# Attention beside a Mish MLP on one core: a stricter rule for ScalarE side jobs, and the row maxima of the two array halves kept level

## The chip, the cores and the metric

The kernel runs on one core of one Trainium2 chip. The metric is device time in microseconds (us), the median of three runs. TensorE (PE in the profile) multiplies, ScalarE (ACT) evaluates functions and copies, VectorE (DVE) reduces and adds, GpSimd (POOL) does elementwise work on data in on-chip memory, and SyncE (SP) issues the DMAs. Each engine works through its own list of instructions in order, and semaphores order the lists against each other.

## The reference

```python
xn = layernorm(x)                               # x: 2048 x 512, D = 512
q = (xn @ wq) in 32 heads of 16;  k = xn @ wk;  v = xn @ wv      # one k and one v for all heads
s = softmax(q k^T / 4) v, heads joined, @ wo
h = xn @ w1 + b1                                # 512 -> F = 1792
g = silu((h * tanh(softplus(h))) @ w2)          # Mish, then back to 512
out = x + s * g
```

All is float32. The softmax needs, for every head and query, the maximum of a row of 2048 scores, and then the exponentials and their weighted sum.

## The kernel before, in words

**Units and steps.** The 2048 queries are cut into 4 chunks of 512 and the 32 heads into 8 groups of 4, so that there are 32 units (chunk, group). A unit takes 16 steps, one for every 128 keys, and there are 512 steps. A head is only 16 deep, and its rows stand several times (high and low parts), so that a score matmul needs 64 of the 128 rows of the TensorE array or fewer: two heads of a unit lie in the lower 64 rows ("side 0") and two in the upper 64 ("side 1"), and a matmul on one side can run beside one on the other.

**What a step issues.** Three kinds of half-array matmul, all of 512 columns:

- "e" (line 1039, in `e_one`): four score tiles, each followed by an exponential on ScalarE (line 1041). In the main loop, all four e of step s lie on the one side 1 - s % 2.
- "m" (line 1060, in `m_one`): score tiles for the row maxima of a unit `LEAD` = 20 steps ahead; VectorE reduces each (line 1064, tile mb). `m_next[0]` and `m_next[1]` count how many have been issued on each side. Four m per step on the average.
- "x" (line 118, in `Mm.half`): the dense layers (queries, w1, w2, wo). Their matmuls are 128 rows deep and are issued as two halves: the halves on side s % 2 in one step, the other halves, on the other side, in the next one. A group of 12 or 15 such matmuls fills one PSUM bank (xps); `chunk_size` cuts it into chunks of at most `XMAX` = 8: 12 into 6 and 6, 15 into 8 and 7. One chunk of k matmuls thus takes two steps. The groups of 15 are those of the second dense layer for the first two of the three parts of F in `THIRDS`, four per chunk of queries and part: 32 in all.

Each step ends with the full-height matmuls "pv" (line 1122), which weigh the values of the step two before; they need all rows.

**How a step is put together.** `m_sides` decides how many of the step's m (`tot` = 4; with odd k, 5 in the chunk's first step and 3 in its second) go to the side of the e (n) and how many to the side of the x (the rest), from k and within limits that keep the two counts at most `MLAG` = 4 apart:

```python
        n = max(min((k + tot - 4) // 2 if k % 2 else k // 2, hi), lo)
        return n, tot - n
```

`em` puts the e and the n m of their side in a row as "MEMEMEME"; `waves` then emits in turn one x of the one side and one e or m of the other, keeps the last of the e side until the last x, and emits the rest of the m, which share the rows of the x, after the x (for odd k after everything). The first x half of the next step waits for the exponential or reduction that followed the last of the other side (`cur["relay"]`), so that the two halves never add into the bank together.

**ScalarE's side jobs.** Beside the exponentials ScalarE evacuates the banks of the dense layers (lines 716, 776, 845) and runs side jobs that wait in the queue `jobs`: the exponentials and logarithms of Mish, of the silu and of the softmax denominators (lines 784, 793, 797, 859, 867, 872, 1146, 1150). `act_jobs` is called once in a step, after the step's e and m. It runs one job, or two when more than two wait; in a step with a bank evacuation on ScalarE (`gap[0]`) it runs one if more than two wait and none otherwise.

**The end.** From step 492 on (`NS - LEAD`) there are no m left. The steps are taken in pairs (`late_pair`), each with eight e and up to two dense groups in "lanes", of each of which 3 to 5 matmuls are done, both halves; `next_group` fills a lane. A group that the main loop left unfinished goes into a lane with what is left of it. After step 512 the last groups and the output follow.

The planning is done when the program is built, with the kernel's own estimates of the times; the engines' lists of instructions are then fixed.

Of the kernel before, what the change touches and what calls it, by code (L numbers as in the profile page):

```python
# [62 lines left out]
def m_need(v):  # L63

    return (34, 64)[v] if v < 2 else 32 * (v + 1)
# [59 lines left out]
def block_kernel(ctx: ExitStack, tc: tile.TileContext, x, wq, wk, wv, wo, w1, b1, w2, out):  # L125
# [169 lines left out]
    def x_high(t):  # L295
        act.activation(x_part(t, 0), xp_of[t], AF.Copy)
# [3 lines left out]
    def x_copy(t):  # L300
        c, tt = divmod(t, 4)
        if tt == 0:
            xf_of[c] = [sb.tile([P, 2, C], F32, tag="act", name=f"xf{c}_{k}", bufs=NACT) for k in range(2)]
        for k in range(2):
            act.activation(xf_of[c][k][:, :, P * tt:P * (tt + 1)], xp_of[t][:, 2 * k:2 * k + 2], AF.Copy)

    def x_low(t):
        sub(dve, x_part(t, 1), xp_of[t], f(x_part(t, 0)))
# [54 lines left out]
    jobs = deque()  # L363
# [5 lines left out]
    gap = [0]  # L369
    ran = [0]  # L370

    def act_jobs(n):
        n = (int(len(jobs) > 2) if gap[0] else n) if n < 9 else n
        gap[0] = 0
        while n > 0:
            k = next((k for k, (fn, free) in enumerate(jobs)
                      if free is None or free() is not None and free() <= step[0]), None)
            if k is None:
                return
            fn = jobs[k][0]  # L380
            del jobs[k]
            fn()
            n -= 1
            ran[0] += 1
# [97 lines left out]
    def pump():  # L482
        for tag in items:
            while arrived(tag):
                split(tag)
            load(tag)
# [3 lines left out]
    cur = {"g": None, "ps": None, "n": 0, "chunk": [], "relay": None}  # L490

    def is_ready(g):
        return (all(i.tile is not None and i.ready <= step[0] + g.slack(k) for k, i in enumerate(g.items))
                and all(d() is not None and d() <= step[0] for d in g.after) and g.pre is None)

    def prepare():
        for n in range(min(2 if step[0] < NS - LEAD else 8, len(queue))):
            if queue[n].pre and queue[n].pre():
                queue[n].pre = None
# [37 lines left out]
    def fill(quota):  # L537
        while quota > 0:
            if cur["g"] is None and not begin():
                return  # L540
            g = cur["g"]
            n = min(quota, len(g.mms) - cur["n"])
            for m in g.mms[cur["n"]:cur["n"] + n]:
                m(cur["ps"])
            cur["n"] += n
            quota -= n
            if finish():
                return
# [3 lines left out]
    lanes = [None, None]  # L552
# [3 lines left out]
    def next_group(z):  # L556

        if cur["g"] is not None:
            lanes[z] = [cur["g"], cur["n"], cur["ps"], None]
            cur["g"] = None  # L560
            return
        prepare()
        if not queue or not is_ready(queue[0]):
            return
        g = queue.popleft()
        if g.start:
            g.start()
        if g.alloc:
            ps = g.alloc(z)
        else:  # L570
            assert not (z and lent)
            ps = late_banks[0] if z else ps_x.tile([P, 512], F32, tag="x", name="xps")
        lanes[z] = [g, 0, ps, None]
# [454 lines left out]
    def e_one(s, i):  # L1028

        v, r = divmod(s, 16)  # L1030
        if s < NS - LEAD:
            a, k, p = 1 - s % 2, r - r % 2 + i // 2, i % 2
        else:
            a, k, p = i % 2, r, i // 2
        q = qt_of[v]
        o = 64 * a
        n_e[0] = (n_e[0] + 1) % (5 if len(lent) < 2 else 4) if late_banks else 0
        e = late_banks[5 - n_e[0]] if n_e[0] > 2 else ps_e.tile([P, C], F32, tag="e", name=f"e{s}_{i}")
        pe.matmul(e, ks[o:o + 64, P * k:P * (k + 1)], q[o:o + 64, p], start=True, stop=True)  # L1039
        pt = sb.tile([P, C], F32, tag="pt", name=f"pt{s}_{i}", bufs=NPT)  # L1040
        r = act.activation(pt, e, AF.Exp, scale=0.25)  # L1041
        pt_of[16 * v + k, p, a] = pt
        return r
# [28 lines left out]
    def m_sides(h, k, second):  # L1072

        tot = 4 + (0 if k % 2 == 0 else -1 if second else 1)
        tot = min(tot, 64 * NU - sum(m_next))
        ahead = m_next[h] - m_next[1 - h]
        lo = max((tot - MLAG - ahead + 1) // 2, tot - (32 * NU - m_next[1 - h]), 0)
        hi = min((tot + MLAG - ahead) // 2, 32 * NU - m_next[h], tot)
        n = max(min((k + tot - 4) // 2 if k % 2 else k // 2, hi), lo)
        return n, tot - n  # L1080

    def c_rows(v):
# [126 lines left out]
    def due(t):  # L1209
        step[0] = t  # L1210
        for k in sorted(k for k in timed if k <= t):
            for fn in timed.pop(k):
                fn()
# [23 lines left out]
    def task(eng, us, fn, deps=(), **kw):  # L1237
        t = Task(eng, us, fn, deps, **kw)
        plan[eng].append(t)
        return t  # L1240
# [57 lines left out]
    for c0, c1 in ((0, 1), (1, 2), (2, 3), (3, 4)):  # L1298
        z = slice(4 * c0, 4 * c1)
# [3 lines left out]
        for c in range(c0, c1):  # L1303
            xs, scs = [], []
            for t in range(4 * c, 4 * c + 4):
# [3 lines left out]
                if c == 0:  # L1309
                    hi = task("ACT", 0.55, lambda t=t: x_high(t), [tr])  # L1310
                    lo = task("DVE", 0.65, lambda t=t: x_low(t), [hi])
# [5 lines left out]
                else:  # L1317
                    lo = task("ACT", 0.62, lambda t=t: x_copy(t), [tr])
# [66 lines left out]
    while True:  # L1385
# [21 lines left out]
        s, e, k = min(opts, key=lambda o: o[0])  # L1407
# [36 lines left out]
        elif k == "J":  # L1444
            tag = next((g for g in ("wq", "ws", "wb") if (g == "wq" or s > 19.0) and arrived(g) and busy[0] + E0 < s + 0.5), None)
            n = ran[0]
# [16 lines left out]
    while left:  # L1463
        k = next(k for k in left if all(d.end is not None for d in k.deps))
# [8 lines left out]
    def pv_to(s):  # L1473

        while pv_next[0] <= s:
            k = pv_next[0]
            pv(k)
            pv_next[0] += 1
            if k % 16 == 15:
                o_out(k // 16)  # L1480
                return

    for s in range(NS + 2000):
        inm = s < NS - LEAD
        if inm or cur["chunk"]:
            assert s < NS
            due(s)
            h = s % 2

            def em(k, second):  # L1490
                n, rest = m_sides(1 - h, k, second) if inm else (0, 0)
                x = deque(lambda i=i: e_one(s, i) for i in range(4))
                y = deque(lambda: m_one(1 - h) for _ in range(n))
                r = [[], []]
                for op in EM if k % 2 == 0 or second else EM[::-1]:
                    if op == "M" and y:
                        r[1 - h].append(y.popleft())
                    elif op == "E":
                        r[1 - h].append(x.popleft())
                r[h] = [lambda j=j: m_one(h, n + rest > 4 and j == rest - 1) for j in range(rest)]  # L1500
                return r

            if s >= 2 and (s - 1) % 16 == 0 and s > 1:
                gap[0] += 1
            waves(h, em, s < NS - LEAD - 1)
            act_jobs(1 + (len(jobs) > 2))
            due(s + 0.5)
            pv_to(s - 2)
        elif s < NS:
            due(s)  # L1510
            if not late_banks:
                late_banks.extend(ps_m.tile([P, C], F32, tag="m", name=f"late{k}") for k in range(3))
                if (NS - s) % 2:
                    for i in range(4):
                        e_one(s, i)
                    fill(4)
                    act_jobs(1)
                    pv_to(s - 2)
                    step[0] = s
                    continue  # L1520
            if (NS - s) % 2 == 0:
                late_pair(s)
            else:
                if s < NS - 3:
                    act_jobs(1)
                pv_to(s - 1)
        else:
            due(s)
            if s == NS:
                act_jobs(2)  # L1530
                pv_to(NS - 1)
                due(s + 0.5)
                lanes_end()
                fill(3)
                fill(3)
            fill(16)
            act_jobs(100)
        step[0] = s
        if vdone[0] < 8 * NC and min(m_next) >= m_need(vdone[0]):
            r = c_rows(vdone[0])  # L1540
            rowq.extend([lambda r=r: (r[0](), behind.append(r[1])),
                         lambda r=r: (r[2](), behind.append(lambda: (r[3](), r[4]())))])
            vdone[0] += 1
        if rowq and not evacs[0]:
            rowq.popleft()()
        while behind and s >= NS - LEAD - 1:
            behind.popleft()()
        evacs[0] = 0
        pump()
        if s > NS + 1 and not queue and cur["g"] is None and not timed and not jobs:  # L1550
            break
# [12 lines left out]
```

## Time and profile before

| | us |
|---|---|
| median of three runs (lowest to highest) | 1581.02 (1580.65 to 1581.16) |
| the profiled execution's own time | 1580.51 |
| its span, first to last instruction | 1578.7 |

| engine | busy in the span, us | share |
|---|---|---|
| TensorE, matmuls | 1566.1 | 99% |
| TensorE, weight loads (beside the matmuls) | 842.6 | 53% |
| VectorE | 1341.9 | 85% |
| ScalarE | 1306.6 | 83% |
| GpSimd | 626.4 | 40% |

In a row of the timeline stand the start in us from the span's start, the length in us, the engine ("PEld" are weight loads), the line, the operation, the tile written and those read, the shapes, the count of instructions merged in the row, and in brackets the idle time before it with what ended it. A row of the waits has the total in us, the number of waits and the longest. A row of the groups has the count, the busy time in us, the mean of one in ns, and the idle time before them.

### The profile page before, as it was taken

The page shows a single profiled execution, that of the slowest core. Times are in us where ns is not written, and L with a number is a line of the kernel's source. Part 1 is how long each engine was busy: PE and PEld are TensorE (multiplying, and loading weights), DVE is VectorE, ACT ScalarE, POOL GpSimd, SP SyncE. Part 2 cuts the span into 40 slices and gives each one's busy share as a digit, 9 for nine tenths or more (in the row PEclk, how much of TensorE's full clock was granted, in tenths as well). Part 3 has the DMA queues.
Part 4 walks back from the last instruction along what each step waited for, and adds up shares of the span by engine and source line. Part 5 has one row for each costly group of instructions (what it writes and reads, how often), then busy time and mean ns, then how long its engine had stood idle before and what let it go on. Part 6 is the DMA issues. An engine that isn't in the chain of part 4 may idle for free.

```text
span 1578.7 us, 31652 instructions
## 1 busy us (share of the span) xinstructions
PE 1566.1 (99%) x11717; PEld 842.6 (53%) x11717; DVE 1341.9 (85%) x2341; ACT 1306.6 (83%) x2515; POOL 626.4 (40%) x641
## 2 busy tenths in 40 slices
PE   9999999999999999999999999999999999999998
PEld 5455555555555555555555555555555555555554
DVE  8998888889889888888898988888889998888832
ACT  7488798798998778978988787897898878789886
POOL 3476266274474104613525131362252414225412
PEclk9999999999999999999999999999999999999999
DMA  6233221132321304222122312220332213032011
GB/s 195 94 117 112 65 100 43 55 125 84 124 91 47 103 15 151 58 71 67 39 79 71 109 61 62 81 71 16 124 98 85 69 54 102 18 111 58 15 58 51
DMA packets 74666, 124.31 MB, mean 79 GB/s; under 512 B 21520, under 2 KB 35344, under 8 KB 74512
## 3 DMA queue, kind: packets, MB, share of 16 engines
q1 hardware_dynamic: 74512, 122.29, 25.1%
q8 instruction: 93, 1.52, 0.4%
q14 instruction: 61, 0.50, 0.1%
HBM read 74.78 MB, written 26.21 MB: 64 GB/s over the span
## 4 chain that ended last, share of the span: by engine, by line
PE 96%; DVE 2%; ACT 1%; DMA 0%; SPq 0%; issue 0%; POOL 0%; ACTq 0%; DVEq 0%
PE xps L118 44%; PE pv L1122 32%; PE e L1039 8%; PE m L1060 8%; DVE mb L1064 2%; PE kp L319 1%; PE xps L114 0%; ACT pt L1041 0%; PE xp L287 0%; PE late L118 0%; DMA xin<-in_dram 0%; PE late L1039 0%; PE wop L114 0%; DVE xt L162 0%; SPq L224 0%
## 5 line engine op out<-in xcount | busy, mean ns | idle before, releaser
L1064 DVE TENSOR_REDUCE mb<-m 128x1 f32<-128x512 f32 x2048 | 1274.0, 683 | 175.0 <-PE m L1060 153.4
L1041 ACT ACTIVATE pt<-e 128x512 f32<-128x512 f32 x2018 | 1061.9, 603 | 219.3 <-PE e L1039 210.6
L1060 PE MATMUL m<-ks,qt 48*128 48x512 f32 (+1 forms) x2048 | 830.5, 421 | 1.7 <-DVE mb L1064 0.8
L1039 PE MATMUL e<-qt,ks 64*128 64x512 f32 x2018 | 741.2, 401 | 0.5 <-ACT pt L1041 0.3
L1122 PE MATMUL pv<-pt,vaug 128*32 128x512 f32 x4096 | 543.0, 604 | 0.0
L1060 PEld LDWEIGHTS m<-ks,qt 48*128 48x128 f32 (+1 forms) x2048 | 372.5, 185 | 63.0 <-DVE mb L1064 25.3
L1039 PEld LDWEIGHTS e<-qt,ks 64*128 64x128 f32 x2018 | 373.3, 186 | 18.5 <-ACT pt L1041 6.7
L118 PE MATMUL xps<-wbs,act 64*128 64x512 f32 x1248 | 338.1, 407 | 0.1
L118 PEld LDWEIGHTS xps<-wbs,act 64*128 64x128 f32 x1248 | 217.6, 185 | 172.2 <-ACT pt L1041 100.7
L118 PE MATMUL xps<-xt,ws 64*128 64x512 f32 x1104 | 306.0, 410 | 0.1
L118 PEld LDWEIGHTS xps<-xt,ws 64*128 64x128 f32 x1104 | 190.2, 185 | 183.2 <-ACT pt L1041 116.5
L172 POOL TENSOR_SCALAR t<-t 128x512 f32<-128x512 f32 x56 | 34.4, 614 | 329.3 <-ACT t L784 328.9
L1122 PEld LDWEIGHTS pv<-pt,vaug 128*32 128x32 f32 x4096 | 81.9, 108 | 136.9 <-issue 128.8
L162 POOL TENSOR_TENSOR hb<-hb,t 128x512 f32<-128x512 f32 x56 | 72.3, 1290 | 64.2 <-ACT t L797 44.1
L118 PE MATMUL xps<-xt,wq 64*128 64x512 f32 x336 | 93.2, 410 | 0.0
L118 PEld LDWEIGHTS xps<-xt,wq 64*128 64x128 f32 x336 | 57.9, 185 | 55.5 <-ACT pt L1041 35.2
L118 PE MATMUL xps<-wbs,ot_all 64*128 64x512 f32 x288 | 79.5, 408 | 0.0
L118 PEld LDWEIGHTS xps<-wbs,ot_all 64*128 64x128 f32 x288 | 49.5, 184 | 46.4 <-ACT pt L1041 30.2
L162 POOL TENSOR_TENSOR hb<-hb,u 128x512 f32<-128x512 f32 x56 | 72.3, 1291 | 4.4
L162 POOL TENSOR_TENSOR u<-u,t 128x512 f32<-128x512 f32 x56 | 71.8, 1282 | 4.7
L162 POOL TENSOR_TENSOR act<-hb,act 128x512 fp32r<-128x512 f32 x55 | 70.8, 1287 | 4.6
L162 POOL TENSOR_TENSOR oc<-oc,sc 128x512 f32<-128x512 f32 (+1 forms) x16 | 20.6, 1288 | 116.5 <-ACT sc L1150 72.0
(146 smaller groups left out, 945.6 us busy)
## 6 DMA issues: line engine op xcount, KB each, us to landing
wbs<-w SPq DMA_DIRECT2D x36, 512.0 KB
ws<-w SPq DMA_DIRECT2D x35, 512.0 KB
qt<-qh SPq DMA_DIRECT2D x256, 32.0 KB
wq<-wq SPq DMA_DIRECT2D x14, 512.0 KB
w<-wbs SPq DMA_DIRECT2D x14, 512.0 KB
wbs<-wo SPq DMA_DIRECT2D x12, 512.0 KB
rawws<-in_dram SPq DMA_DIRECT2D x21, 256.0 KB
rawwb<-in_dram SPq DMA_DIRECT2D x20, 256.0 KB
```

The costliest lines, as they stand in the source:

```text
L118: i = self.pe.matmul(ps, self.lhs()[o], self.rhs()[o], start=(self.k == 0 and self.halves == 0), stop=(self.k == self.tot - 1 and self.hal ...
L162: eng.tensor_tensor(out=o, in0=a, in1=b, op=op)
L172: pool.tensor_scalar(o, o, lim, 0.0, op0=ALU.min, op1=ALU.max)
L319: pe.matmul(kp_of[c], wkf[:, dt], xf_of[c][dt // 2][:, dt % 2], start=(dt == 0), stop=(dt == 3))
L1039: pe.matmul(e, ks[o:o + 64, P * k:P * (k + 1)], q[o:o + 64, p], start=True, stop=True)
L1041: r = act.activation(pt, e, AF.Exp, scale=0.25)
L1060: pe.matmul(m, q[o, p, P * t:P * (t + 1)], ks[o, C * kb:C * (kb + 1)], start=True, stop=True)
L1064: r = dve.reduce_max(out=mb_of[v][:, kb, z:z + 1], in_=m, axis=AX.X)
L1122: pe.matmul(o[32 * j:32 * j + 32], vaug[:, k], pt, start=(k == 0), stop=(k == 15))
```

## The change

Three things are changed. First, in `act_jobs` and at its call in the main loop, "more than two wait" becomes "more than three wait". Second, `m_sides` gets a correction: n is first chosen as before; then it is worked out by how much the step would leave the side of its e ahead in m, less two where the e are on side 1 (h = 1 in `m_sides`) and nothing where they are on side 0; where a chunk of x is in the step (k > 0) and this differs from zero by more than one, n is moved by one towards it. Third, a group that goes from the main loop into a lane takes along the instruction for which its next half has to wait.

```diff
     def act_jobs(n):
-        n = (int(len(jobs) > 2) if gap[0] else n) if n < 9 else n
+        n = (int(len(jobs) > 3) if gap[0] else n) if n < 9 else n
...
     def next_group(z):
...
         if cur["g"] is not None:
-            lanes[z] = [cur["g"], cur["n"], cur["ps"], None]
+            lanes[z] = [cur["g"], cur["n"], cur["ps"], cur["relay"]]
...
     def m_sides(h, k, second):
...
-        n = max(min((k + tot - 4) // 2 if k % 2 else k // 2, hi), lo)
+        n = (k + tot - 4) // 2 if k % 2 else k // 2
+        off = ahead + 2 * n - tot - 2 * h
+        if k and abs(off) > 1:
+            n -= 1 if off > 0 else -1
+        n = max(min(n, hi), lo)
         return n, tot - n
...
             waves(h, em, s < NS - LEAD - 1)
-            act_jobs(1 + (len(jobs) > 2))
+            act_jobs(1 + (len(jobs) > 3))
             due(s + 0.5)
             pv_to(s - 2)
```

## The prediction

> **What bounds the kernel now.** I read the page first: the busy shares, the granted clock and the chain of waits.
>
> ```profile
> span 1578.7 us, 31652 instructions
> PE 1566.1 (99%) x11717; PEld 842.6 (53%) x11717; DVE 1341.9 (85%) x2341; ACT 1306.6 (83%) x2515; POOL 626.4 (40%) x641
> PEclk9999999999999999999999999999999999999999
> PE 96%; DVE 2%; ACT 1%; DMA 0%; SPq 0%; issue 0%; POOL 0%; ACTq 0%; DVEq 0%
> ```
>
> TensorE is in the chain for 96% of the span, at full clock, and is almost never without a matmul. That a matmul is always running doesn't yet say that both halves of the array are in use, so the next thing to read is the timeline of single steps. A step's end shows as its pv row (x8); the distance of two such rows is a step. Here are two ordinary steps (six x halves) and the two after them:
>
> ```profile
> 747.32 1.07 PE L1122 MATMUL pv<-pt,vaug 128*32 128x512 f32 x8
> 750.12 0.68 ACT L776 ACTIVATE hb<-xps,b1c 128x512 f32<-128x512 f32 x1
> 750.17 1.06 PE L1122 MATMUL pv<-pt,vaug 128*32 128x512 f32 x8
> 751.64 0.74 ACT L793 ACTIVATE t<-u,two 128x512 f32<-128x512 f32 x1
> 752.25 2.08 ACT L1041 ACTIVATE pt<-e 128x512 f32<-128x512 f32 x4
> 753.35 1.06 PE L1122 MATMUL pv<-pt,vaug 128*32 128x512 f32 x8
> 756.34 1.07 PE L1122 MATMUL pv<-pt,vaug 128*32 128x512 f32 x8
> ```
>
> The first takes 2.85 us. The second takes 3.18 and the third 2.99: ScalarE had an evacuation and a side job behind one step's exponentials, then more jobs, and the exponentials start late. That is the stall the job rule is about. Now a stretch with chunks of eight, in which one step happens to be lopsided:
>
> ```profile
> 538.05 1.06 PE L1122 MATMUL pv<-pt,vaug 128*32 128x512 f32 x8
> 540.09 0.39 PE L118 MATMUL xps<-wbs,act 64*128 64x512 f32 x1
> 540.09 0.39 PE L1039 MATMUL e<-qt,ks 64*128 64x512 f32 x1
> 540.09 0.42 PEld L118 LDWEIGHTS xps<-wbs,act 64*128 64x128 f32 x2
> 540.32 0.39 PE L118 MATMUL xps<-wbs,act 64*128 64x512 f32 x1
> 540.55 0.63 PE L118 MATMUL xps<-wbs,act 64*128 64x512 f32 x2
> 541.02 0.63 PE L1060 MATMUL m<-ks,qt 48*128 48x512 f32 x2
> 541.45 1.29 DVE L1064 TENSOR_REDUCE mb<-m 128x1 f32<-128x512 f32 x2 [0.55 <-PE m L1060]
> 541.58 1.06 PE L1122 MATMUL pv<-pt,vaug 128*32 128x512 f32 x8
> ...
> 544.32 0.39 PE L118 MATMUL xps<-wbs,act 64*128 64x512 f32 x1
> 544.33 0.40 PE L1039 MATMUL e<-qt,ks 64*128 64x512 f32 x1
> 544.65 0.64 PE L1122 MATMUL pv<-pt,vaug 128*32 128x512 f32 x4
> ```
>
> Two starts that belong together (540.09, one on each side) are a slot; the next starts 0.23 us later (540.32, 540.55). Starts on one side with no partner also take 0.23 each. The step from 541.58 to 544.65 has eight x against four e and four m, eight slots, 3.07 us. An ordinary one has six x and one m against four e and three m, seven slots, 2.85 us: one slot less, 0.22 less. The step from 538.05 to 541.58 has the limit of `MLAG` at work: n = 2, so ten half matmuls (eight x, two m) against six. It lasts 3.53 us: two slots more, 0.46 more. So a step's price is 1.24 us (pv and the edges) plus 0.23 us times the longer side's count.
>
> The whole loop agrees:
>
> ```profile
> 86.71 1.06 PE L1122 MATMUL pv<-pt,vaug 128*32 128x512 f32 x8
> 89.55 1.06 PE L1122 MATMUL pv<-pt,vaug 128*32 128x512 f32 x8
> ...
> 475.17 1.06 PE L1122 MATMUL pv<-pt,vaug 128*32 128x512 f32 x8
> ...
> 478.08 0.64 PE L1122 MATMUL pv<-pt,vaug 128*32 128x512 f32 x4
> ...
> 1506.02 1.06 PE L1122 MATMUL pv<-pt,vaug 128*32 128x512 f32 x8
> 1509.42 1.06 PE L1122 MATMUL pv<-pt,vaug 128*32 128x512 f32 x8
> ```
>
> From the first row to the last are 489 steps and 1422.7 us. Four are without x (two of them 2.91 us, ending at 478.08, and 3.40, ending at 1509.42; the other two 2.71), together 11.7 us. The other 485, counted by the code's rule, are 391 of seven slots, 92 of eight, one of six and one of ten: 3489 slots. 485 x 1.24 + 3489 x 0.23 = 1403.9 us, against 1411.0 measured. All stalls of the loop on other engines are thus about 7 us, and that is the most that smoother side jobs can win.
>
> **The level rule, which is the large term.** With six x the old n (3) makes the sides differ by two and by nothing in turn, which is what the rule wants: off is 0. With seven, off is 1 or less: left alone. With eight, n = 4, and off = 0 + 8 - 4 - 2 = 2 on side 1, and the same from the other side in the next step (-2 + 8 - 4 - 0 = 2): n becomes 3. A step that had eight against eight now has seven (four e, three m) against nine (eight x, one m). The order of the changed program's instructions shows it: x7 and x8 stand together, then the last e, then one m on the rows of the x, then pv. Nine slots for eight, and no matmul fewer.
>
> How many: 31 of the 32 groups of fifteen begin in the loop, each with a chunk of eight over two steps, 62 steps of which one is the lopsided one. In the changed program's order all 32 begin there, 64 steps: 62 with nine slots, one with ten, one with eight. 62 x 0.23 = **+14.3 us**. What could cover it: nothing on TensorE, since pv needs all rows and follows the ninth slot. The m moved from the seventh slot to the ninth is reduced 0.46 us later, but VectorE is behind TensorE by less than a step:
>
> ```profile
> L1064 DVE TENSOR_REDUCE mb<-m 128x1 f32<-128x512 f32 x1962 | 1221.0, 683 | 172.3 <-PE m L1060 151.1 <-PE xps L118 19.4 <-PE e L1039 0.2
> ```
>
> Four of 683 ns are 2.73 us in a step that now lasts 3.30. In the ten-slot step two reductions ended after pv had begun (541.45 + 1.29), and the next still took 3.07. The fourth e stays in slot eight, so ScalarE and the wait of the next x for its exponential (`cur["relay"]`) are no later against the step's end.
>
> **The other corrections.** After the first empty step three steps of six x are moved by one, eight slots for seven: 3 x 0.23 = **+0.7**. The two steps of four x at the very start get seven slots for six; the second of them, from 86.71 to 89.55 in the rows above, already takes 2.84, as long as seven slots, so I take nothing (two slots, 0.5, at most).
>
> **A group that moves.** In the changed order the loop has two empty steps instead of four, and two more steps of chunks of eight (3.07 each; their ninth slot is in the 62). Out go 2.91 + 3.40 = 6.3, in come 6.1: **-0.2**.
>
> **The job rule.** Seven steps of the loop have two jobs, seven an evacuation and a job; afterwards none and three. The place shown costs 3.18 + 2.99 - 2 x 2.85 = 0.47. Counting the pv distances, the like places lose 2.0 us in all (two of 0.47, four of 0.24, one of 0.13), and the three that remain, at 0.24, 0.7: **-1.3**. A job later by a step could delay a group, but by the changed order none is: the loop does one group more, not less, and the side jobs are the same 248.
>
> **The last 20 steps.** One lane begins with a group of which eight matmuls are done, so three pairs have four matmuls in a lane where they had five: one slot less in each of two halves. From the rows of the scores that open a pair:
>
> ```profile
> 1516.57 0.50 PE L1039 MATMUL e<-qt,ks 64*128 64x512 f32 x1
> ...
> 1521.85 0.49 PE L1039 MATMUL e<-qt,ks 64*128 64x512 f32 x1
> ...
> 1532.16 0.50 PE L1039 MATMUL late<-qt,ks 64*128 64x512 f32 x2
> ...
> 1537.02 0.49 PE L1039 MATMUL e<-qt,ks 64*128 64x512 f32 x2
> ```
>
> a pair with a lane of five takes 5.28, one with four 4.86: 3 x 0.42 = -1.3 at most, nothing if the eight exponentials (some 0.6 each) and a job set the pair. I take **-1.1**. The lane that is carried over has a new wait, for an exponential of the step before, with all of TensorE behind it. The loop has this wait at every chunk, and it costs TensorE next to nothing there:
>
> ```profile
> PE xps L118 <- ACT pt L1041: 0.3, 1, 0.3
> ```
>
> so 0, and one exponential, 0.6, at most.
>
> **Sum.** 14.3 + 0.7 - 0.2 - 1.3 - 1.1 = +12.4 us. On the profiled execution's 1580.5 (span 1578.7 and 1.8 around it) that is 1592.9; the median lies 0.5 above that execution, so **1593.4 us**, 0.8% slower. Bounds: if every stall in the loop vanished (-7.1 for the -1.3), 1587.6; with nothing won from jobs and lanes and 0.6 + 0.5 lost at the lane and the four-x steps, 1596.9.
>
> **Rivals.**
>
> *The ninth slot is hidden.* ScalarE's exponentials would have to set the end of a step of eight, not the slots: four exponentials (2.1) and a job (0.74) are 2.8 of 3.07. Then the first term is 0, the sum -1.9, and the time 1579.1: no slower than before. It decides if a ninth slot costs under 0.08 us (62 x 0.08 = 5, less 1.9, is 0.2% of the time, about what a measurement of this kernel can tell from no change). Against it: two extra slots cost 0.46 in the one lopsided step, and eight slots cost just one more than seven. With the stalls of the steps of seven gone too (another 2), it would be 1577, faster. Chance 0.05, of it 0.02 faster.
>
> *Partly hidden.* The longer steps give ScalarE and VectorE time to catch up, and the steps after them run at the bare price; 0.15 to 0.2 us a slot net. 62 x 0.16 = 9.9, the sum about +8, 1589. For it: some steps of seven take up to 0.1 over the price. Chance 0.13.
>
> *Weights on the same side can't load under a matmul.* x8 follows x7, and m follows x8, on the same rows with nothing between; if the load (0.18 us a row) had to wait for the running matmul, an extra slot would cost 0.41, and the sum would be 62 x 0.18 = 11.2 more: 1604.6. Against it: in the lopsided step two loads on the same rows take 0.42 together, under the running x, whose starts stay 0.23 apart. The Trainium skill ("TensorE: Matmul & The Clock Gate", Part 3) says that a weight load overlaps with running matmuls only where the row group differs; this trace disagrees. Chance 0.03.
>
> *The delayed jobs come back as stalls*, at the lanes or after step 512, where a job is waited for. Two or three exponential-sized jobs, 2 us: 1596. The jobs left at step 510 are one in both orders. Chance 0.05, in the range.
>
> The forecast itself has 0.74, with its own range 1590 to 1596. The range for 8 in 10 takes in the partly hidden case and late jobs: **1587 to 1597**. Faster 0.02, the same 0.04, slower 0.94.
>
> **What will show it.** Right: pv rows 3.30 apart in the steps of eight x, with an unpaired x and an unpaired m in each; 2.85 in the steps of six; busy time per engine but for TensorE unchanged; the first pv of the last 20 steps some 13 us later. Wrong: pv rows still 3.07 apart there (the ninth slot is free), or 3.5 (loads don't overlap); a new idle time of TensorE ended by a side job's line; or a last part longer than the 69 us from 1509.42 on.

## The result, and the profile after

The changed kernel takes 1593.43 us (median of six runs, 1593.16 to 1593.79) against 1581.03 before: ratio 1.0073, 95% interval 1.0059 to 1.0087. The forecast was 1593.4, in a range of 1587 to 1597.

The page of the changed kernel's profile, its span, its busy shares, its granted clock and the chain by engine:

```profile
span 1591.7 us, 31648 instructions
PE 1579.7 (99%) x11717; PEld 853.3 (54%) x11717; DVE 1346.3 (85%) x2339; ACT 1307.5 (82%) x2515; POOL 627.3 (39%) x641
PEclk9999999999999999999999999999999999999999
PE 96%; DVE 2%; ACT 1%; DMA 0%; SPq 0%; issue 0%; ACTq 0%; DVEq 0%
```

The same 11717 matmuls keep TensorE busy for 13.6 us longer; their weight loads, beside them, 10.7; no other engine has grown by more than 4.4. That is what slots without a partner look like on a page: as many matmuls, a longer union of their times, and not more idle time (12.6 us of the span before, 12.0 after). The timeline shows where. It is the end of one step of eight x and the whole of the next (the columns are those of the timelines before):

```profile
125.31 1.06 PE L1126 MATMUL pv<-pt,vaug 128*32 128x512 f32 x8
...
127.35 0.42 PEld L118 LDWEIGHTS xps<-wbs,act 64*128 64x128 f32 x2
127.56 0.39 PE L1039 MATMUL e<-qt,ks 64*128 64x512 f32 x1
127.58 0.40 PE L118 MATMUL xps<-wbs,act 64*128 64x512 f32 x1
127.80 0.45 PE L1039 MATMUL e<-qt,ks 64*128 64x512 f32 x1
127.81 0.63 PE L118 MATMUL xps<-wbs,act 64*128 64x512 f32 x2
128.28 0.39 PE L1060 MATMUL m<-ks,qt 64*128 64x512 f32 x1
128.61 1.07 PE L1126 MATMUL pv<-pt,vaug 128*32 128x512 f32 x8
...
131.58 0.39 PE L1060 MATMUL m<-ks,qt 64*128 64x512 f32 x1
131.90 1.06 PE L1126 MATMUL pv<-pt,vaug 128*32 128x512 f32 x8
```

The row at 127.81 is two x, 0.23 us apart, and the m at 128.28 starts 0.24 after the second: the ninth slot, with the other side empty. pv follows it. The steps last 3.30 and 3.29 us.

The engine's waits are as short as before; no wait has taken the place of another. The first row is of the kernel before, the other two of the changed kernel:

```profile
PE m L1060 <- DVE mb L1064: 0.8, 3, 0.3
...
PE m L1060 <- DVE mb L1064: 0.5, 1, 0.5
PE xps L118 <- ACT pt L1041: 0.3, 1, 0.3
```

Put together from the pv rows of the two profiled executions (1578.7 and 1591.7 us of span):

| part of the span | before, us | after, us | difference |
|---|---|---|---|
| to the first pv | 86.7 | 87.9 | +1.2 |
| 489 steps of the loop | 1422.7 | 1436.3 | +13.6 |
| last 20 steps, to the last pv | 54.5 | 53.1 | -1.4 |
| from the last pv to the end | 14.8 | 14.4 | -0.4 |

Within the loop: the 62 steps of nine slots take 3.302 us on the average, where steps of eight x and eight slots took 3.084: 62 x 0.218 = +13.5. The three corrected steps of six x take 3.09 for 2.86, +0.7. The group that moved: two steps of eight x (6.2) for two without x (5.9), +0.3. The one step of four x in this stretch, +0.4. The rest, -1.3, is what the stalls of the loop have become less.

### The profile page after: what moved, and what is told of

It is laid out like the page before. It is cut to its first block, busy times and chain, and to the rows that moved or that the text cites. A ratio compares the mean times of both kernels' runs of the same rounds, so it can differ in the third digit from the quotient of the medians.

```text
span 1591.7 us, 31648 instructions
## 1 busy us (share of the span) xinstructions
PE 1579.7 (99%) x11717; PEld 853.3 (54%) x11717; DVE 1346.3 (85%) x2339; ACT 1307.5 (82%) x2515; POOL 627.3 (39%) x641
## 4 chain that ended last, share of the span: by engine, by line
PE 96%; DVE 2%; ACT 1%; DMA 0%; SPq 0%; issue 0%; ACTq 0%; DVEq 0%
PE xps L118 46%; PE pv L1126 32%; PE m L1060 8%; PE e L1039 7%; DVE mb L1064 2%; PE kp L319 1%; ACT pt L1041 1%; PE late L118 1%; PE xps L114 0%; PE xp L287 0%; DMA xin<-in_dram 0%; PE late L1039 0%; PE late L114 0%; PE wop L114 0%; DVE xt L162 0%
## 5 line engine op out<-in xcount | busy, mean ns | idle before, releaser
L1039 PE MATMUL e<-qt,ks 64*128 64x512 f32 x2018 | 732.1, 401 | 0.5 <-ACT pt L1041 0.3
L157 POOL TENSOR_SCALAR qh<-qf 128x512 fp32r<-128x512 f32 x15 | 9.3, 621 | 106.0 <-ACT qf L716 80.0
```

The costliest lines, as they stand in the source:

```text
L157: pool.tensor_scalar(o, i, 1.0, 0.0, op0=ALU.mult, op1=ALU.add)
```

## The experiments

All times are medians; the kernel before took 1580.92 us beside the first four and 1580.75 beside the last three.

**The level correction left out in steps of eight x.** Against the changed kernel:

```diff
-        if k and abs(off) > 1:
+        if 0 < k < 8 and abs(off) > 1:
```

> The changed kernel with the level correction left out in the steps of eight x, and only there. In its order all 62 steps with nine slots have eight again; 3538 slots against 3600; everything else stands in the same steps. Theory: 62 x 0.22 = 13.6 less than the changed kernel, 1579.8 us. Rival (the ninth slot is hidden): no change, 1593. Rival (half hidden, the rest is from the other corrections): 1586 to 1588.

Measured: 1580.11 us (ten runs, 1579.25 to 1580.48), 13.3 less than the changed kernel; ratio to the kernel before 0.9994 (0.9985 to 1.0004), no change that can be told. 13.3 / 62 = 0.215 us a slot, of the 0.23 between two starts: the ninth slot was paid almost in full, and it is the whole loss.

**Two slots without a partner.** The kernel before with the third change, and in place of the correction:

```diff
+        if k == 8:
+            n -= 2
```

> The kernel before with n = 2 in every step of eight x: six half matmuls on the side of the e, ten on the side of the x, so two slots without a partner in each of 62 steps and one or two in a step of seven x; the order of all else is that of the kernel before. Theory (every slot without a partner costs the same 0.22 to 0.23, first or second): 62 x 2 x 0.22 = 27.3 more than before, 1608.3 us (1609.6 at 0.23). Rival (weights on the same side can't load under a running matmul, so that a slot without a partner costs 0.4): 1631. Rival (one slot is covered by ScalarE's and VectorE's slack and only the next is paid): +14, 1595.

Measured: 1608.26 us, +27.3, as the first theory has it. The steps of ten slots take 3.54 us, 0.46 over those of eight. Neither the first nor the second slot is covered, and loading weights under a running matmul on the same rows costs nothing extra; 1595 and 1631 are both excluded.

**The level correction alone** (the changed kernel with "more than two" for the jobs):

```diff
-        n = (int(len(jobs) > 3) if gap[0] else n) if n < 9 else n
+        n = (int(len(jobs) > 2) if gap[0] else n) if n < 9 else n
...
-            act_jobs(1 + (len(jobs) > 3))
+            act_jobs(1 + (len(jobs) > 2))
```

> The changed kernel with the old job rule (more than two wait); the level correction alone. In its order 60 steps of eight x have nine slots, one step of seven x has nine for eight, the two steps of four x at the start have seven for six, and nothing else moves. Theory: 60 x 0.22 + 0.2 + 0.2 + 0.8 at the start = +14.4, about 1595.4 us, 2 more than the changed kernel. Rival (late jobs are the cause): near 1581. Rival (the longer steps win time back on ScalarE where the old job rule stalls): 1593 or less.

Measured: 1593.65 us, the same as the changed kernel and 1.8 under what was expected. The stalls of the loop (its 489 steps' times less 1.24 + 0.23 for each slot, steps without x left aside) are 5.5 us here and 7.1 before. At 0.22 us a slot, which the kernel of ten slots gives, the difference is 1.0 and not 1.6. Either way some time comes back with the longer steps, as the third possibility said. Beside the level correction the job rule is worth 0.2 us between the medians and 0.7 between the two profiled executions (1594.18 and 1593.44).

**The job rule alone** (the changed kernel without the correction):

```diff
-        if k and abs(off) > 1:
-            n -= 1 if off > 0 else -1
```

> The changed kernel without the level correction (n as before the change); the job rule (more than three) and the carried lane stay. In its order the loop has 3534 slots against 3526 before, two steps without x instead of four, no step with two jobs, and three with an evacuation and a job instead of seven. Theory (slots at 0.23 us plus small gains): two more steps of eight (+6.1), two of the steps without x less (-6.1), one slot each in two steps (+0.5), stalls -2.0, last 20 steps and what follows -1.9: about 1577.7 us, some 3 less than before. Rival (the change is slow because delayed side jobs hold groups up, not because of the slots): near 1593, since all jobs are as late here as in the changed kernel.

Measured: 1587.28 us (1585.39 to 1588.29), ratio 1.0039 (1.0024 to 1.0054): slower than before, where a gain of 3 had been expected. The rival as written (jobs hold groups up) isn't it either: the groups stand in the same steps as in the kernel of the first experiment, which takes 1580.1. The waits of TensorE name another cause, new in this kernel:

```profile
PE e L1039 <- DMA qt<-cr: 5.0, 3, 1.7
```

Three times the first scores of a unit wait for the transfer that writes the unit's row maxima into its query tile. The timeline at the first of them (unit 9, whose first step follows the pv at 495.06):

```profile
486.41 0.68 DVE L162 TENSOR_TENSOR y<-xps,y 128x512 f32<-128x512 f32 x1
...
490.59 0.25 DVE L1091 TENSOR_REDUCE mp<-mb 128x16 f32<-128x64 f32 x1
...
494.38 0.20 DVE L1103 STREAM_TRANSPOSE cr<-mp 128x32 f32<-128x32 f32 x1
...
494.61 5.31 SPq L1111 DMA_DIRECT2D qt<-cr  x8
...
495.06 1.07 PE L1124 MATMUL pv<-pt,vaug 128*32 128x512 f32 x8
...
498.49 0.46 PE L1039 MATMUL e<-qt,ks 64*128 64x512 f32 x1 [1.71 <-DMA qt<-cr]
```

The maxima are put together at 490.59 and turned at 494.38; eight DMA issues follow, which take 5.3 us; the unit's step begins at 496.06, and its first e starts at 498.49, 3.9 after the first issue. The step takes 5.00 us. Those of units 13 and 15 take 6.17 and 4.98: with this one 7.6 over three ordinary ones. The wait is nearly the same in all three (1.71, 1.62 and 1.68); the step of unit 13 is longer because TensorE's granted clock fell behind the wait. Its slots are 0.42 to 0.43 us apart, and the next step takes 3.28. In these rows (units 9 and 13) stand a stretch and its length, the busy time of the five engines, the granted clock, the DMA engines' share and GB/s:

```profile
495.06:500.06 5.00, 3.29 (x24) 1.61 (x22) 2.82 (x6) 2.06 (x6) 0.00 (x0) 1.00 0.03 6
685.21:691.38 6.17, 4.55 (x24) 2.38 (x22) 3.33 (x7) 2.01 (x5) 0.00 (x0) 0.76 0.02 3
```

So a part of the loss in this execution is lost clock, some 1.2 us in the step. It may also be why the four executions lie so far apart: at 1585.39 and 1586.53 us the mean clock is 0.999, at 1588.29 and 1588.04 it is 0.996; only the first has a trace. In the kernel without the correction in steps of eight x, the same unit's first step begins after the pv at 497.15:

```profile
486.85 0.27 DVE L1093 TENSOR_REDUCE mp<-mb 128x16 f32<-128x64 f32 x1
488.48 0.68 DVE L162 TENSOR_TENSOR y<-xps,y 128x512 f32<-128x512 f32 x1
...
493.62 0.20 DVE L1105 STREAM_TRANSPOSE cr<-mp 128x32 f32<-128x32 f32 x1
493.85 5.31 SPq L1113 DMA_DIRECT2D qt<-cr  x8
...
497.15 1.07 PE L1126 MATMUL pv<-pt,vaug 128*32 128x512 f32 x8
```

There the issues begin 4.3 us before the unit's step (493.85 to 498.15), not 1.5 (494.61 to 496.06): the last maximum comes a step earlier, so that the maxima are begun before the addition y out of the bank, not after. The order agrees: `rowq` is held back in a step that ends such an addition (`evacs[0]`). With an odd number of steps without x, the chunks begin in the other kind of step, and the last maximum of a unit comes four steps ahead of the unit instead of five; where the next step also holds the queue back, it is too late. Neither is enough alone: in the kernel before, units 11 to 30 have the short lead too, units 5 and 7 are held back, their issues begin 4.1 to 4.5 us ahead of their steps, and none of them waits. Two ways to lose this lead are told apart by the next two kernels.

**The sides level also without x.** The job rule alone, and

```diff
+        if k == 0 and step[0] < 480:
+            n = 2
```

> The kernel with the job rule alone, and with n = 2 in the two steps without x, so that no step leaves the sides further apart than an ordinary one. In its order there is no step of nine or ten slots, the last maximum of units 9 to 21 still comes four steps ahead of the unit's first scores (five in the changed kernel), and in units 9, 13 and 15 the step that would begin the writing of the maxima into the query tile (line 1109 before the change) is one with an addition out of a bank on VectorE, which puts it off by one more step. Theory A (the phase: the row of maxima starts a step later, and a step later again behind the addition): the stalls at the first scores of units 9, 13 and 15 stay, 7 to 8 us, and the time is that of the job rule alone, 1585 to 1588 us. Theory B (the sides are four apart, and that is what holds the maxima up): the stalls go, 1578 to 1580.

Measured: 1589.57 us (1586.23 to 1589.87), with three waits for the same transfer. Theory A stands for the waits: how far the sides are apart isn't their cause. Its figure is exceeded by 1.6 us. Two things were left out of it. Each of the two steps without x takes 3.40 us here, where it takes 2.70 with the job rule alone: +1.4. And the clock fell behind all three waits, not one. At unit 9 the step with the wait and the next one are:

```profile
495.81:501.30 5.49, 3.79 (x25) 1.78 (x23) 3.28 (x7) 2.42 (x6) 0.00 (x0) 0.89 0.03 6
501.30:505.20 3.90, 3.90 (x24) 1.79 (x23) 2.61 (x6) 1.83 (x5) 1.27 (x1) 0.71 0.45 137
```

The three steps with a wait and the three after them take 28.3 us here, 25.1 in the profiled execution of the job rule alone.

**The maxima not held back.** The job rule alone, and

```diff
-        if rowq and not evacs[0]:
+        if rowq:
```

> The kernel with the job rule alone, and with one condition dropped in the main loop: the maxima of a finished unit are put together and written (the queue rowq) also in a step with an addition out of a bank on VectorE, instead of waiting for the next step. No matmul, job or slot moves. Theory A (the write of the maxima is late by the step it is put off): the waits for the transfer at units 9, 13 and 15 go, 8 us less than the job rule alone, 1577 to 1579 us. Rival (the transfer itself is slow there, or the issue queue full): 1585 or more. Rival (VectorE, with the addition and the maxima in one step, holds up TensorE instead): 1580 to 1583.

Measured: 1578.48 us (eleven runs, 1577.98 to 1579.36), 8.8 less than the job rule alone; ratio to the kernel before 0.9987 (0.9978 to 0.9996). The waits for the transfer are gone. The timeline at unit 9, whose first step follows the pv at 495.60:

```profile
486.77 0.68 DVE L162 TENSOR_TENSOR y<-xps,y 128x512 f32<-128x512 f32 x1
...
488.57 0.25 DVE L1091 TENSOR_REDUCE mp<-mb 128x16 f32<-128x64 f32 x1
...
492.08 0.20 DVE L1103 STREAM_TRANSPOSE cr<-mp 128x32 f32<-128x32 f32 x1
492.31 5.30 SPq L1111 DMA_DIRECT2D qt<-cr  x8
...
495.60 1.06 PE L1124 MATMUL pv<-pt,vaug 128*32 128x512 f32 x8
```

The maxima are put together 1.8 us after the addition begins, not 4.2, and the issues begin 4.3 us before the unit's step. With the waits the fall of the clock behind them is gone as well. This version is faster than the changed kernel and, by 0.13%, than the kernel before; it lies near the 1577.7 us that had been expected of the job rule alone.

**The level correction in steps of fewer than eight x, from the fifth step on.**

```diff
-        if k and abs(off) > 1:
+        if 0 < k < 8 and step[0] > 4 and abs(off) > 1:
```

> The changed kernel with the level correction only in steps of fewer than eight x and from the fifth step on: three steps of six x have eight slots, and nothing else is corrected. Theory: the kernel without the correction in steps of eight (1580.1), less 0.8 us for the two steps of four x at the start, which then are as before: 1579.3 us, 1.7 less than before the change. If the first scores still come 0.7 us later in the span than before the change, that part of the start is not the correction's. Rival (the corrections at the start cost nothing, the start differs from run to run): 1580.1.

Measured: 1579.08 us (eleven runs), 1.0 less than with the two steps at the start; 0.9992 (0.9983 to 1.0001) of the kernel before. In the profiled executions the two steps at the start take 0.8 us less (0.44 and 0.35). The first scores come 0.85 us earlier besides, at 78.43 us of the span, and a wait for weights in one later step (3.62 us) takes some 0.5 back. So of the 1.0 us it isn't shown how much is the correction's and how much the earlier start's.

## Why the prediction was right, point by point

- *The sum, +12.4.* Between the two profiled executions the time grew by 12.9 us (1580.51 to 1593.44), their spans by 13.0. That the forecast meets the median to the tenth is luck: the errors of the terms below (-0.8, +0.5, -0.7, +1.6) nearly cancel, and the median before lay 0.5 above its profiled execution, the median after did not.
- *The ninth slot, +14.3.* Right in mechanism and nearly in size: 13.5 in the trace, 13.3 between two kernels that differ in this alone. The price read off one lopsided step and off the difference between seven and eight slots held for all 62.
- *The other corrections, +0.7.* Right for the three steps of six x (+0.7). For the steps of four x at the start the forecast took nothing, with 0.5 at most, because the second of them was already as long as seven slots; this term was mis-sized, and the two lose 0.8. Another 0.75 is lost ahead of them (the last point below). The pv rows of the changed kernel

```profile
87.90 1.07 PE L1126 MATMUL pv<-pt,vaug 128*32 128x512 f32 x8
91.12 1.06 PE L1126 MATMUL pv<-pt,vaug 128*32 128x512 f32 x8
```

 are 3.22 apart, 0.38 more than before, and the step ahead loses another 0.45. An m has moved ahead of the third e there. The m have three banks, so the fourth m of these steps waits for a reduction, and the e wait behind it. In the first of the two steps VectorE reduces without a pause; in the second it had been idle for 0.7 us before, and the m simply come faster than it reduces them:

```profile
86.48 1.03 PE L1060 MATMUL m<-ks,qt 64*128 64x512 f32 x2
...
87.35 0.62 PE L1039 MATMUL e<-qt,ks 64*128 64x512 f32 x2
...
89.93 0.79 PE L1060 MATMUL m<-ks,qt 64*128 64x512 f32 x2
90.56 0.63 PE L1039 MATMUL e<-qt,ks 64*128 64x512 f32 x2
```

 What the prediction didn't see is that a step pays for the order of its m, and not only for its slots, where VectorE has no slack to give the banks back in time.
- *The group that moves, -0.2.* +0.3 in the trace: the two steps without x that are left take 2.70 and 3.18 us, not the 2.71 that the forecast took for each.
- *The job rule, -1.3.* The stalls of the loop are some 1.3 less, as forecast, but not for the reason given: with the level correction alone they are already 1.0 to 1.6 less, and the job rule adds 0.2 to 0.7 to that. So the size is right in part by luck. And the sentence that a later job delays nothing was argued for the groups alone. The job rule also moves the steps without x, with them the kind of step in which a chunk begins, and through it the lead of the row maxima. Alone it costs 6.4 us; the level correction, in the three steps of six x after the first step without x, brings the lead back to five steps and takes 7.2 of this away (1587.28 to 1580.11). The forecast's sum holds since it was made for both together; split by halves of the change it would have been wrong for this one. It didn't look at the lead of the row maxima, so that the other half repairs it was luck too.
- *The last 20 steps, -1.1.* -1.4, and another -0.4 after the last pv. The first three pairs give 1.3 of it (4.00, 5.67 and 4.91 us for 4.43, 6.15 and 5.28), which is the term's upper bound. The carried lane's wait doesn't show.
- *The rivals.* The hidden ninth slot would have given 1579 and is excluded by both slot experiments. The partly hidden one fits a little: the stalls are 1.0 to 1.6 less in the kernel with the level correction alone, 0.02 to 0.03 us a slot. Of a load that can't run under a matmul on the same rows there is no trace: the loads of two x at 127.35 take 0.42 together, under running x.
- *Still open.* In the three executions with the correction in the first steps the first e comes at 79.28 to 79.36 us of the span, in the six without it at 78.43 to 78.90. The engines' instructions up to there are in the same order; the difference is there from the first loads of the input on: VectorE begins with the third piece of x at 6.16 to 6.29 us in the three, at 5.26 to 5.74 in the six. Each kernel has one profiled execution, and no run tells why.

## What to carry to other kernels

Where two half-array streams share TensorE and a full-height matmul closes each step, the step costs the longer stream: a rule that shifts one matmul from one side to the other, for whatever good reason, costs a whole slot (0.22 us here) every time both sides were equal. Look for the steps that are lopsided already; one of them prices all others. And before saying that a later side job delays nothing, follow what moves with it: here the parity of a chunk's first step and a bookkeeping condition (hold the row back behind an addition) decided together whether a row of maxima was begun 4.3 or 1.5 us before it was needed, and dropping the condition was worth 8.8 us; half a change can look harmless only because its other half repairs it.

## What the runs showed of the hardware that was not expected

Eight DMA issues for 2 x 8 x 32 elements each keep SyncE's queue for 5.3 us, close to two steps, and from the first issue to the first e that needs them 3.9 us pass. So a late decision on VectorE comes out as a wait of TensorE when the issues begin 1.5 us before the unit's step (1.7 us of wait), and doesn't at 4.1 us or more; none of the units 1 to 30 lies between in any trace.

Waits of TensorE of 1.6 to 1.7 us can cost more than themselves: the granted clock fell behind one of the three in one profiled execution (0.76 over the step of unit 13) and behind all three in another (0.71 to 0.89), with up to 1.2 us more for the step and 1.0 for the next. Behind two waits just as long it stayed at 1.00; the runs don't show what decides this.
